# Values term of chunks 2 to 5 in 128x32 tiles, values loaded once more, tokens put in order at the eviction of y

## The chip, the cores and the metric

One core of one Trainium2 chip runs the kernel. The metric is the device time in microseconds (us), the median of repeated runs; lower is better. A profile shows one execution from the first to the last instruction (its span). The engines are named as in the profile: PE (TensorE matmuls), PEld (TensorE weight loads), DVE (VectorE), ACT (ScalarE), POOL (GpSimd), SP (SyncE, which here only issues DMAs).

## The reference

A gated linear attention over 768 tokens, for 4 batch rows and 8 heads of width 48, feeds a bilinear feed-forward layer over its 3072 tokens:

```python
for t in range(S):
    state = alpha[:, :, t, :, None] * state + np.einsum('bhd,bhe->bhde', k[:, :, t], v[:, :, t])
    y[:, :, t] = np.einsum('bhd,bhde->bhe', q[:, :, t], state)
...
a = x @ w_a        # x: y of all heads side by side, 3072 x 384; w_a, w_b: 384 x 1536
b = x @ w_b
return (a * b @ w_out).astype(np.float32)
```

## The kernel before

**Chunks.** The work is cut into 6 chunks. A chunk is 256 tokens of 2 batch rows (u = 0, 1). Partition p holds the tokens 2p and 2p + 1 (called rank 0 and 1), so that a load has runs of 96 elements. The 256 tokens are two blocks of 128 (g = 0, 1), which lie on the partitions 0 to 63 and 64 to 127. The recurrence goes from block to block by a 48x48 state per head; inside a block it is written with matrices.

**The attention part of a chunk.** Logarithms of alpha (step ln) and their running sums give the decays: pair sums on POOL (L613, l2s), their split into parts on DVE (L623, R), the sums on PE (L633, AQ), exponentials on ACT (L667, E); the decay over a whole block comes for chunks 0 and 1 from small matmuls (`decay_pe`, L700). `mul` (L678, steps mq and mk) multiplies queries and keys by them into `QKp`. For chunks 2 to 5, `turn_dma` (L767, step T) transposes `QKp` into `kqT` with a DMA that SP issues. `scores` (L841, step D) makes keys times queries on PE in 64x64 tiles: output half g of the partitions, and in it 64 keys of one rank. `masked` (L846, M) or `unmasked` and `masked_in_place` (L850 and L854, Mc and Mm) turn them into the masked tile `m`. `state_pe` and `state_pe_both` (L799 and L812, K and K2) make keys times values, and `state` (L829, L830, k) updates the state. The output y of a batch row collects in two PSUM banks: `carried` (steps SB and SA) adds queries times old state, and `inner` (Y) adds values times `m`. Both go through `out_mm` (L865) in 64x64 tiles. `inner` takes 48 matmuls a batch row: 12 pieces of heads, 2 ranks, 2 blocks. It reads the values from `vx`, a copy of the loaded values that `vcast` (L785 on ACT, L787 on DVE, step v) spreads to 96 columns a head. `evac` (L900, L902, step X) copies y of one batch row, 128x768, from PSUM to `xT`. The 128 tokens of a block stand there with the even ones first.

**The feed-forward part.** `ff` (L919, steps a and b) multiplies 128 columns of w_a or w_b with `xT`, for one batch row (256 tokens) or both (`*`, 512 tokens), in three matmuls. `ff_as` (L925, as) copies a's product to SBUF; `ff_prod` (L933, pr) multiplies it with b's product, and its output pattern (`tokens`) puts the tokens back in order. `ff_o` (L941, o) multiplies with w_out, `ff_out` (L956, L958, ot) evicts, `store` (L974, st) writes to memory.

**The order of the work** is written by hand: the text `PROGRAM` lists all steps, each with its chunk, its arguments, a PSUM bank and the engine (V is DVE, S is ACT, P is POOL, Y is SP). Each engine carries out its own steps in the order of the text and waits for the data of others. PE's order mixes the attention of one chunk with the feed-forward part of the one before. SP issues transposes, some loads and all stores; POOL issues the other loads, among its own arithmetic (L613, L652). Loads have two buffers for each of q, k, v and alpha, and are issued one to two chunks ahead.

Of the kernel before, what the change touches and what calls it, by code (L numbers as in the profile page):

```python
# [41 lines left out]
0: b 2 1 0; pr 2 1; a 6 * 3; as 4 1; b 1 1 2
1: l2 1 V
0: pr 4 1; as 6 *
1: H 1 V
0: pr 1 1
1: A2 0 7
0: a 11 * 0; a 7 * 5; a 0 1 4
1: L 1 V
0: k 1 1 V  # L50
1: ra 1
0: as 11 *
1: lv 0 q V; E 0 i
0: as 0 1; b 6 * 0; b 11 * 3; a 8 * 4; pr 6 *; pr 11 *
2: ld a * P
0: b 0 1 1; as 8 *; a 3 1 6
1: E 0 b; lv 0 k V
0: a 10 * 2; pr 0 1
1: mq 0 V; ld v 1 P
0: b 8 * 4  # L60
1: A2 1 7
0: as 10 *; b 10 * 2; pr 8 *
1: E 1 b
0: as 3 1; as 7 *; b 9 * 3; b 3 1 0; b 7 * 1; a 9 * 6
2: ld q * P
1: v 0 S; lv 1 q V; mk 0 V
0: pr 10 *
1: mq 1 V; C 0 1 4
0: as 9 *
1: C 0 0 2  # L70
0: o 0 0 5; pr 7 *
1: dk * 6
2: ld k * P
3: ld v * P
0: cz 1 v P; pr 9 *
1: Ce 0 0 S; E 1 i; de *; lv 1 k P; Ce 0 1 V; D 0 1 1; D 0 0 3
0: pr 3 1
1: Mc 0 0; K2 0 0 7 0
0: o 1 0 6
1: mk 1 V; M 0 1  # L80
0: o 3 0 4; o 1 1 -; ot 1 S; c3 P
3: ld a * P
0: cs 1 0 P; o 3 1 -
1: k 0 0 V; k 0 1 V; Mm 0 0 V; SB 0 1; C 1 0 3; C 1 1 7
0: ot 3 S; o 0 1 -
1: Ce 1 0 V
2: ln *
1: v 1 V; D 1 0 3; Ce 1 1 S; K2 1 1 6 0; Y 0; SA 0
0: ot 0 V
1: k 1 0 V; D 1 1 6  # L90
0: o 2 0 5
1: M 1 0
2: l2 0 V
1: X 0 S; a 3 0 1; Mc 1 1
2: l2s 0 P; l2s 1 P
1: a 2 0 3; a 4 0 4
2: R 0
1: k 1 1 V; as 4 0
2: ra 1
1: as 3 0; b 4 0 7  # L100
0: o 2 1 -
1: as 2 0
0: ot 2 S
1: pr 4 0
2: R 1; lv 1 q P
1: b 3 0 6; b 2 0 7; a 5 0 2; pr 3 0; b 5 0 3; as 5 0; b 1 0 5; a 1 0 1; pr 5 0; pr 2 0; a 7 0 2; as 1 0; pr 1 0
2: AQ 3
1: SB 1 6
2: lv 0 k P
1: a 10 0 5  # L110
2: lv 1 k V; ra 0; ld v * P
1: Mm 1 1 V
2: E 1 b
1: as 10 0; b 10 0 0; pr 10 0
2: mq 1 V; E 1 i
1: as 7 0; b 7 0 1
2: E 0 b; E 0 i
1: a 0 0 5
0: st 3 Y
2: dr  # L120
1: SA 1; Y 1
2: mk 1 V
1: pr 7 0; a 11 0 0; a 6 0 3; b 6 0 2; X 1 S; b 11 0 4; a 2 1 6; as 6 0; a 3 1 7; as 11 0; b 2 1 1; pr 6 0
2: lv 0 q V
1: b 4 1 0; as 2 1
2: T 1
1: pr 11 0
2: dl
0: st 0 Y
1: a 0 1 2; pr 2 1  # L130
2: mq 0 V
1: b 3 1 3; b 0 0 6; as 3 1; as 0 0; b 0 1 7; pr 3 1; a 8 0 1; a 9 0 5
0: st 1 Y
1: b 8 0 3; b 9 0 4; pr 0 0; as 0 1
2: mk 0 V
1: a 4 1 2
3: ln *
1: a 9 1 6; pr 0 1; as 8 0; b 9 1 1
3: ra 1
1: b 10 1 7; pr 8 0; a 10 1 3; as 4 1; as 9 0; as 9 1; a 6 1 6; b 6 1 2; b 11 1 5; pr 4 1; as 10 1; pr 9 0; a 11 1 4; pr 10 1; pr 9 1; as 6 1  # L140
2: v 1 S
1: a 8 1 3; b 8 1 1; a 7 1 6; pr 6 1
3: l2 0 V
1: as 11 1
2: T 0
1: as 8 1; a 5 1 4
3: ra 0
1: as 5 1; a 1 1 2
2: v 0 V
4: ld a * Y  # L150
1: pr 11 1; as 7 1; pr 8 1
2: K2 * * 0 7; D 1 1 3; D 1 0 5
1: as 1 1; b 5 1 2; o 2 0 1
2: k * 0 V
1: pr 5 1
3: v 0 S; v 1 S
1: b 1 1 2
2: Mc 1 0; M 1 1
3: l2s 0 P; l2s 1 P
1: b 7 1 0; o 2 1 -; pr 1 1; o 3 0 4  # L160
# [12 lines left out]
0: cs 0 0 P
2: Mc 0 1
4: ln *
3: ld q * Y; ld k * Y
2: k * 1 V
3: AQ 2
2: Y 1; SA 1; Mm 0 1 V; Mm 0 0 V; Y 0; X 0 S
3: E 0 b  # L180
4: l2 0 V
2: X 1 V
1: o 0 1 -
2: b 1 * 6; a 1 * 5
3: E 1 b
4: ld k * Y
3: E 1 i
1: ot 0 S
3: E 0 i
4: l2s 0 P  # L190
2: a 0 * 0; b 0 * 1; as 0 *; as 1 *
3: lv 0 k P; lv 0 q P
2: a 5 * 7
1: st 3 Y
2: a 7 * 4
4: l2s 1 P
2: a 2 * 5
3: lv 1 q V; mq 1 V; lv 1 k V
2: pr 1 *
3: dr  # L200
2: pr 0 *
3: mk 0 V
4: ld q * Y
0: st 2 Y
2: as 5 *; a 6 * 6; b 6 * 2; as 7 *
3: mq 0 V
2: b 9 * 4; b 7 * 0
1: st 2 Y
3: dl
4: R 0  # L210
2: b 5 * 7
1: o 1 0 3
2: a 9 * 1; pr 7 *; as 6 *
3: T 0
2: pr 6 *
4: ra 0
2: pr 5 *; a 11 * 6
3: mk 1 V
2: as 9 *; a 3 * 0
4: lv 0 k V; lv 0 q V; R 1  # L220
2: as 2 *
1: o 1 1 -
2: as 11 *; a 8 * 5; b 11 * 2; a 4 * 7; b 2 * 1
3: T 1
1: ot 1 V
2: pr 9 *; as 8 *; pr 11 *; pr 2 *; b 8 * 3; b 4 * 5; as 4 *
5: ld a * Y
3: K2 * * 4 6
2: pr 8 *; as 3 *; pr 4 *
3: k * 0 V; D 0 0 2; Mc 0 0  # L230
2: b 3 * 1
4: ra 1
2: pr 3 *; b 10 * 5; a 10 * 0
3: D 1 0 1; D 1 1 3
2: as 10 *
3: k * 1 V; Mc 1 1
2: o 0 0 7; o 2 0 0
3: M 1 0
5: ln *
2: pr 10 *  # L240
4: lv 1 q P
3: SB 1 3; D 0 1 1; Mc 0 1
4: lv 1 k P
5: ld q * Y
1: st 0 Y
3: SB 0 5
2: o 2 1 -
3: Mm 1 1 V; Mm 0 0 V; Mm 0 1 V
4: ld v * P
2: ot 2 S; o 0 1 -  # L250
4: AQ 0; E 0 b; E 0 i
3: SA 0; Y 0; SA 1
4: E 1 b
3: Y 1
5: l2s 1 V
4: mq 0 V; mk 0 V
3: X 0 S; X 1 S
2: o 3 0 2; o 3 1 -
4: T 0
3: a 5 * 3  # L260
4: E 1 i; v 0 S
3: a 9 * 0
2: ot 3 S
3: b 5 * 6; a 6 * 5; as 5 *
2: st 2 Y
3: as 9 *
5: ld k * P; l2s 0 P
3: as 6 *
5: ra 1
4: mq 1 V  # L270
2: ot 0 S
3: a 0 * 1
4: mk 1 V
3: a 1 * 2
4: D 0 0 3
5: l2 0 V
1: st 1 Y
4: dr
5: R 0
3: pr 5 *  # L280
4: v 1 S; M 0 0
3: b 1 * 7; as 1 *; a 3 * 5; b 9 * 6; pr 9 *; b 6 * 4; a 2 * 0; pr 6 *
4: T 1
5: lv 0 k P
3: b 0 * 6; as 0 *; as 2 *
4: dl
3: a 8 * 1
5: lv 1 q P
3: b 4 * 0; a 4 * 4; b 2 * 3; pr 1 *; pr 0 *; as 8 *; pr 2 *; as 4 *; pr 4 *; b 3 * 6; b 8 * 2
5: ld v * P; lv 1 k P  # L290
3: a 11 * 1
5: ra 0
3: as 3 *; pr 8 *; as 11 *; a 7 * 0
4: D 1 0 3; K * 0 5
5: lv 0 q P
3: pr 3 *; as 7 *
5: v 1 V
4: k * 0 V
# [106 lines left out]
def kernel(  # L405
# [14 lines left out]
    C = 128  # L420
# [678 lines left out]
```

## Time and profile before

| | |
|---|---|
| runs | 193.73, 194.18, 194.41 us; median 194.18 |
| span of the profiled execution | 192.0 us |
| first matmul starts, last one ends | 1.19 us, 188.65 us |
| DVE busy, ACT busy, POOL busy | 133.1, 106.5, 56.9 us |
| packets of DMA | 62618 in all, 18432 of them in POOL's queue |
| last load that lands | 120.2 us (values of chunk 5) |

The span is shorter than the time of a run, which holds the launch too: 2.2 us lie between the span and the median. "Busy" of PE counts the modelled time of a matmul from start to end, several at once; how fast PE advances is read from the starts, and matmuls of different tiles that start within a few ns of each other run side by side. A line of groups gives the line in the kernel, the engine, what it writes and reads with shapes, how often, busy time, mean time of one, and the idle time before.

### The profile page before, as it was taken

To read this page: it belongs to the slowest core of one execution; us is meant where nothing else is said; L and a number is where in the kernel's file an instruction comes from. 1 tells how busy PE (TensorE), PEld (TensorE's weight loads), DVE (VectorE), ACT (ScalarE), POOL (GpSimd) and SP (SyncE) were. 2 spreads that over 40 slices of the span, in tenths; PEclk is the share of its full clock that TensorE was granted. 3 is DMA by queue.
4 is the path that set the end of the run, shared out by engine and by line. 5 is a ranking of instruction groups with operands and counts; after the bars stand their busy time and mean duration, and the time that the engine had idled before them with its cause. 6 is when DMAs were issued, how large, how long until landed. Compare 5 with 4: busy or idle time off the path is not lost.

```text
span 192.0 us, 6086 instructions
## 1 busy us (share of the span) xinstructions
PE 186.8 (97%) x2613; PEld 116.9 (61%) x2613; DVE 133.1 (69%) x223; ACT 106.5 (55%) x194; POOL 56.9 (30%) x75
## 2 busy tenths in 40 slices
PE   7999999999999999999999999999999999999992
PEld 3888875677778876645557444656465644545562
DVE  2387698994989888899897956887567446252510
ACT  4448885656779867753487756743572435314211
POOL 8999626752450500640074262000000000000000
PEclk9999999999999999999999999999999999999999
DMA  5999999999969999999999989017641200000422
GB/s 132 274 219 218 251 253 235 244 269 264 251 107 166 165 216 265 248 254 149 233 213 181 156 174 129 3 42 140 146 66 44 85 0 0 0 0 3 164 82 82
DMA packets 62618, 29.40 MB, mean 153 GB/s; under 512 B 53712, under 2 KB 60768, under 8 KB 62592
## 3 DMA queue, kind: packets, MB, share of 16 engines
q0 software_dynamic: 18432, 13.37, 39.6%
q1 hardware_dynamic: 44016, 15.55, 38.1%
q8 instruction: 20, 0.33, 0.7%
q10 hardware_dynamic: 144, 0.10, 0.2%
q14 instruction: 6, 0.05, 0.1%
HBM read 25.98 MB, written 4.74 MB: 160 GB/s over the span
## 4 chain that ended last, share of the span: by engine, by line
PE 91%; DMA 5%; SPq 1%; DVE 1%; issue 1%; ACT 0%; DVEq 0%
PE psum L919 47%; PE psum L941 24%; PE psum L865 7%; PE psum L841 3%; DMA kqT<-QKp 3%; DMA q_t<-in_q_dram 3%; PE psum L736 2%; PE psum L633 1%; PE psum L952 1%; SPq L549 1%; PE psum L799 1%; PE psum L812 1%; PE psum L700 1%; PE psum L591 1%; PE psum L592 1%
## 5 line engine op out<-in xcount | busy, mean ns | idle before, releaser
L919 PE MATMUL psum<-xT,wb_t 128*128 128x512 bf16 (+1 forms) x270 | 56.0, 337 | 0.0
L919 PE MATMUL psum<-xT,wa_t 128*128 128x512 bf16 (+1 forms) x270 | 56.0, 337 | 0.0
L941 PE MATMUL psum<-wo_t,prod 128*128 128x384 bf16 x276 | 49.4, 326 | 0.0
L919 PEld LDWEIGHTS <-wb_t 128*128 128x128 bf16 x270 | 25.9, 98 | 19.9 <-issue 0.5
L919 PEld LDWEIGHTS <-wa_t 128*128 128x128 bf16 x270 | 25.9, 98 | 19.7 <-issue 0.3
L941 PEld LDWEIGHTS <-prod 128*128 128x128 bf16 x276 | 25.9, 98 | 17.6
L956 ACT ACTIVATE ot<-psum 128x384 f32<-128x384 f32 (+1 forms) x16 | 7.7, 482 | 22.7 <-PE psum L941 21.6
L850 ACT ACTIVATE m<-psum 128x1024 bf16<-128x1024 f32 x14 | 14.1, 1023 | 4.6 <-PE psum L841 4.3
L613 POOL TENSOR_TENSOR l<-la 64x384 f32<-64x384 f32 x7 | 7.8, 1108 | 26.6 <-ACT la L556 19.0
L846 DVE TENSOR_TENSOR m<-psum,mask 128x1024 bf16<-128x1024 f32 x10 | 12.1, 1220 | 3.1 <-PE psum L841 3.1
L652 POOL TENSOR_TENSOR q_t<-q_t,ra 128x384 f32<-128x384 f32 x5 | 6.1, 1215 | 22.5 <-ACT ra L645 19.7
L556 ACT ACTIVATE la<-a_t 128x1536 f32<-128x1536 f32 (+2 forms) x9 | 9.5, 1055 | 2.3 <-DMA a_t<-in_alpha_dram 2.2
L678 DVE TENSOR_TENSOR QKp<-q_t,beta 128x768 bf16<-128x768 f32 x10 | 10.0, 995 | 1.0 <-ACT beta L667 1.0
L865 PE MATMUL psum<-m,vx 64*64 64x128 bf16 x576 | 10.5, 217 | 0.0
L900 ACT ACTIVATE xT<-psum 128x768 bf16<-128x768 f32 x9 | 7.2, 816 | 5.7 <-PE psum L865 5.5
L678 DVE TENSOR_TENSOR QKp<-k_t,invb 128x768 bf16<-128x768 f32 x10 | 9.7, 972 | 0.8 <-ACT invb L667 0.8
L854 DVE TENSOR_TENSOR m<-m,mask 128x1024 bf16<-128x1024 bf16 x14 | 9.3, 684 | 1.2 <-ACT m L850 1.2
L958 DVE COPY ot<-psum 128x384 f32<-128x384 f32 (+1 forms) x9 | 4.8, 532 | 7.6 <-PE psum L941 4.7
L865 PEld LDWEIGHTS <-vx 64*64 64x64 bf16 x576 | 9.0, 107 | 0.5 <-issue 0.3
L841 PE MATMUL psum<-kqT 64*64 64x128 bf16 x384 | 9.0, 219 | 0.4 <-DMA kqT<-QKp 0.3
L652 POOL TENSOR_TENSOR k_t<-k_t,a_t 128x384 f32<-128x384 f32 x6 | 7.4, 1228 | 6.1 <-issue 3.3
L549 POOL DMA_DIRECT2D v_t<-in_v_dram x8 | 8.5, 1058 | 0.1
(271 smaller groups left out, 287.9 us busy)
## 6 DMA issues: line engine op xcount, KB each, us to landing
out_dram<-ot SPq DMA_DIRECT2D x23, 192.0 KB, 3.8
q_t<-in_q_dram SPq DMA_DIRECT2D x3, 768.0 KB, 6.5
a_t<-in_alpha_dram POOLq DMA_DIRECT2D x2, 768.0 KB, 15.2
k_t<-in_k_dram POOLq DMA_DIRECT2D x2, 768.0 KB, 12.1
v_t<-in_v_dram POOLq DMA_DIRECT2D x4, 384.0 KB, 7.0
a_t<-in_alpha_dram SPq DMA_DIRECT2D x2, 768.0 KB
k_t<-in_k_dram SPq DMA_DIRECT2D x2, 768.0 KB
a_t<-in_alpha_dram POOLq DMA_DIRECT2D x3, 384.0 KB, 8.5
```

What stands on the lines that cost most here:

```text
L549: eng.dma_start(out=t[:, us, hs].rearrange("p b h r d -> p (b h) (r d)"), in_=src[ch.b0 + us.start:ch.b0 + us.stop, hs, ch.s * 2 * C:(ch.s ...
L556: nc.scalar.activation(out=ch.la[:, us, hs].rearrange("p b h r d -> p (b h r d)"), in_=ch.a[:, us, hs].rearrange("p b h r d -> p (b h r d) ...
L613: eng.tensor_add(ch.l2[(1 - g) * HC:(2 - g) * HC, 1], x[:, :, 0, :], x[:, :, 1, :])
L652: eng.tensor_mul(x, x, by)
L678: eng.tensor_mul(QKp[ch.c % 2][:, u, j, :, hs, :D], src[:, u, hs].rearrange("p h r d -> p r h d"), f)
L841: nc.tensor.matmul(s2[g * HC:(g + 1) * HC, r, p, rk, :], lhsT=turned_part(ch, u, 1, rk, 2 * h + p, g, rs), rhs=queriesT(ch, u, 2 * h + p, ...
L846: nc.vector.tensor_mul(m.rearrange("p r a k s -> p (r a) (k s)"), ch.s2[u, h].rearrange("p r a k s -> p (r a) (k s)"), maskn(4))
L850: nc.scalar.activation(out=m.rearrange("p r a k s -> p (r a) (k s)"), in_=ch.s2[u, h].rearrange("p r a k s -> p (r a) (k s)"), func=AF.Copy)
L854: eng.tensor_mul(x, x, maskn(4))
L865: nc.tensor.matmul(y[c * DP:(c + 1) * DP, g, j // 2 * C:(j // 2 + 1) * C], lhsT=lhsT, rhs=rhs, start=(g, c) not in begun, stop=False, skip ...
L919: nc.tensor.matmul(p, lhsT=(wa_t, wb_t)[w][:, kk, f * 128:(f + 1) * 128], rhs=ch.xT[:, kk, us, :], start=(kk == 0), stop=(kk == KT - 1))
L941: nc.tensor.matmul(op, lhsT=ch.prod[:, f, at:at + C], rhs=wo_t[:, f, :], start=(f == 0), stop=(f == NFF - 1))
```

## The change

1. For chunks 2 to 5 (`NR = 2`), the scores are laid out so that all 128 keys of a block stand on the 128 partitions (rank 0 on 0 to 63, rank 1 on 64 to 127). `inner_rows` then takes both ranks in one matmul of 128 rows and 32 columns: 32 a batch row instead of 48. `scores` issues the same matmuls in another order of rank and block; the masks use a table `mask2`, made once on POOL (step cm2).
2. The values in that order are loaded once more (`load_rows`, step lw): four DMAs a chunk, issued by POOL, each for one block and one rank, with runs of 48 elements. They land in the memory of `vx`, seen as `vps` with 64 columns a head, whose padding is set to zero once (cz w). The state matmuls of these chunks read the loaded values directly, and `vcast` goes away for them.
3. `evac` now takes one block, 128x384, and writes its tokens in order; `xT` has the block as its outer index. `ff_prod` writes straight through.
4. `PROGRAM` is written anew: the same steps, but for those above, in another order, with other banks and partly other engines.

```diff
+    VP = D + DP // 2
+    NR = 2
...
+    mask2 = cst.tile([C, 2, HC], BF16, name="mask2")
+    vps = [t.rearrange("p b r h e -> p (b r h e)")[:, :4 * H * VP].rearrange("p (g b h e) -> p g b h e", g=2, b=2, h=H) for t in vxs]
...
+    def const_mask2(eng):
+        for rk in range(2):
+            ks = slice(rk * HC, (rk + 1) * HC)
+            ENG[eng].tensor_copy(mask2[ks], mask[ks, rk])
...
+    def load_rows(ch, g, rk, eng):
+        at = ch.s * 2 * C + g * C
+        eng.dma_start(out=vps[ch.c % 2][rk * HC:(rk + 1) * HC, g, :, :, :D].rearrange("p b h d -> p (b h) d"),
+                      in_=v[ch.b0:ch.b0 + 2, :, at:at + C, :].rearrange("b h (s r) d -> r s (b h) d", r=2)[rk])
...
+    def values(ch, gs, u, rk, hd):
+        return ch.v[gs, u, hd, rk, :] if ch.c >= NR else vxs[ch.c % 2][gs, u, rk, hd, :D]
...
+    SLICES = [(h, 3 * (h // 2) + j) for h in range(H) for j in ((0, 1) if h % 2 == 0 else (1, 2))]
+    RANKS = [[x for x in SLICES if x[1] % 4 == c] for c in range(4)]
+
+    def inner_rows(ch, u):
+        y, begun = ch.y[u]
+        vp = vps[ch.c % 2].rearrange("p g b h e -> p g b (h e)")
+        W32 = DP // 2
+        for n in reversed(range(len(SLICES) // 4)):
+            for g in range(2):
+                for c in range(4):
+                    h, j = RANKS[c][n]
+                    at = h * VP + W32 * j - D * h
+                    assert (g, c // 2) in begun
+                    nc.tensor.matmul(y[c * W32:(c + 1) * W32, g, j // 4 * C:(j // 4 + 1) * C], lhsT=vp[:, g, u, at:at + W32],
+                                     rhs=ch.m[u, h // 4][:, h % 2, h // 2 % 2, g, :], start=False, stop=False, skip_group_check=True)
...
-    def evac(ch, u, eng):
+    def evac(ch, u, g, eng):
         if not hasattr(ch, "xT"):
-            ch.xT = wk.tile([128, KT, B, C], BF16, name="xT")
-        o_ = ch.xT[:, :, 2 * u:2 * u + 2, :].rearrange("p a g s -> p g a s")
-        i_ = ch.y[u][0][:, :, :KT * C].rearrange("p g (a s) -> p g a s", a=KT)
...
+            ch.xT = wk.tile([128, B, KT, C], BF16, name="xT")
+        evict(ch.xT[:, 2 * u + g].rearrange("p a (s r) -> p a r s", r=2),
+              ch.y[u][0][:, g, :KT * C].rearrange("p (a r s) -> p a r s", a=KT, r=2), eng)
...
-        o_, a_, b_ = tokens(ch.prod[:, f, :], us), columns(a[:, :n], n), columns(b, n)
-        nc.vector.tensor_mul(o_, a_, b_)
+        nc.vector.tensor_mul(ch.prod[:, f, us.start * C:us.stop * C], a[:, :n], b)
```

The steps of the attention of chunk 3 in the new text, for example (steps of other chunks between them are left out):

```
3: lw 0 0 P
...
3: lw 0 1 P; lw 1 0 P
...
3: lw 1 1 P
...
3: l2s 0 P; l2s 1 P; R 0
...
3: AQ 2
...
3: ld q * Y
...
3: E 1 i; lv 1 q V; E 1 b; mq 1 V; E 0 b
...
3: ld k * Y; lv 0 k P; mk 0 V; lv 1 k V; mk 1 V
...
3: lv 0 q P; mq 0 V; dl
3: K2 * * 2 5
...
3: T 0
...
3: T 1
...
3: D 0 1 2; D 1 1 4; Mc 1 1; D 1 0 6; M 1 0
```

More of the change, by code (lines that the diff above doesn't have):

```diff
@@ L95 @@
[L95 to L100, printed above, removed]
+0: cz 1 v P
+1: mq 0 V
+0: b 10 * 0
+1: E 0 i; ra 1
+0: as 3 1; a 9 * 2; a 4 1 4; as 10 *; pr 10 *
+1: v 0 S; lv 0 k V; mk 0 V
+0: a 7 * 6
+1: de *
+0: a 11 * 5
+1: lv 1 q V
+0: pr 3 1; b 11 * 0; as 11 *; pr 11 *
+1: A2 1 1; E 1 b; C 0 0 5; E 1 i; mq 1 V; Ce 0 0 V
+0: as 4 1; b 7 * 7; b 4 1 0; pr 4 1; as 7 *; pr 7 *; b 9 * 1; as 9 *
+1: lv 1 k P; mk 1 V
+0: pr 9 *; a 6 * 4; as 6 *
+1: C 0 1 2; Ce 0 1 S; D 0 0 5; Mc 0 0; K2 0 0 0 7
@@ new lines @@
+0: pr 6 *
+1: k 0 0 V; k 0 1 V
+0: o 0 0 4; o 3 0 2
+1: D 0 1 5; Mm 0 0 V
+0: c3 P
+3: ld a * P
+1: SB 0 0
+2: ln *; ra 1
+1: C 1 0 3; Ce 1 0 V; M 0 1
+2: ra 0
+1: C 1 1 7; Ce 1 1 V
+0: cs 1 0 P; o 0 1 -; o 3 1 -; ot 3 V; st 3 Y
+1: D 1 0 5; Y 0; M 1 0; SA 0; X 0 1 S
+0: ot 0 S
+1: D 1 1 2; Mc 1 1
+0: o 1 0 7; o 2 0 1
+1: X 0 0 V; a 1 0 0; as 1 0
+2: l2s 0 P
+1: b 7 0 6; b 1 0 2
+0: o 1 1 -; ot 1 S
+2: l2 0 V; l2s 1 P
+0: st 0 Y
+2: R 0; R 1; AQ 4; E 0 b
+1: pr 1 0
+2: E 0 i
+1: v 1 V; K2 1 1 0 2; k 1 0 V
@@ L197 @@
[L197 to L202, printed above, removed]
+2: D 0 0 4; Mc 0 0
+3: l2s 0 P; l2s 1 P; R 0
+2: M 1 1
+1: o 0 1 -; ot 0 S; pr 9 1; o 2 1 -; ot 2 V
+2: D 0 1 2; Mc 0 1
+3: R 1
+2: SB 1 4; SB 0 6; Mm 0 0 V; Mm 0 1 V
+1: a 11 1 0; as 11 1; o 3 0 1; b 11 1 0; pr 11 1
+2: SA 0; SA 1
+3: AQ 2
+4: ln *; l2 0 V
+2: Y 1; Y 0; X 0 0 S
+1: o 1 0 0; o 1 1 -
+2: X 1 0 V
+1: o 3 1 -
+2: X 0 1 V; X 1 1 V; b 11 * 4
+3: ld q * Y
+2: a 11 * 5
+3: E 0 i
+0: cs 0 0 P
+4: l2s 0 P
@@ L241 @@
+2: a 1 * 3; b 1 * 1
+3: k * 0 V
+2: as 1 *; pr 1 *; as 0 *; b 4 * 4
+1: ot 1 V
+2: b 6 * 2; pr 6 *
+4: ra 1; l2s 1 P
+3: T 0
+4: R 0
+3: k * 1 V
+2: a 7 * 6; a 10 * 0; pr 0 *
+3: T 1
+2: b 10 * 1; a 4 * 2; as 10 *; pr 10 *; b 7 * 3; as 7 *; pr 7 *
+5: ld a * Y
+2: as 4 *; a 8 * 5; as 8 *; pr 4 *; a 9 * 0; as 9 *
+4: ra 0
+2: b 8 * 1; pr 8 *
+1: st 2 Y
+3: D 0 1 2; D 1 1 4; Mc 1 1; D 1 0 6; M 1 0
+2: b 9 * 0
 4: lv 1 q P
-3: SB 1 3; D 0 1 1; Mc 0 1
+2: pr 9 *
 4: lv 1 k P
 5: ld q * Y
-1: st 0 Y
@@ new lines @@
+5: ln *
+4: ld v * P; R 1; AQ 6; E 0 b
+3: Mm 1 1 V
+4: lv 0 k V
+3: SA 0
+1: st 0 Y
+3: SA 1
+4: E 0 i
+3: Mm 0 0 V; Y 0
+4: lw 0 0 P
+3: X 0 1 S
+4: lv 0 q V; mq 0 V
+3: Y 1
+2: o 3 0 6; o 3 1 -
+3: X 1 0 V; X 0 0 S; X 1 1 V; a 5 * 2; as 5 *
+4: E 1 b
+3: a 8 * 3
+5: l2 0 V
+3: b 6 * 4
+4: lw 0 1 P
+2: ot 2 S
+4: E 1 i
+2: ot 3 S
+4: lw 1 0 P
+3: a 6 * 2; as 6 *
+5: l2s 1 V
+3: b 1 * 1
+4: lw 1 1 P
+3: b 5 * 5
+4: mk 0 V; T 0
+5: ld k * P
+4: mk 1 V
+3: as 8 *; pr 6 *; pr 5 *; a 3 * 2; as 3 *
@@ L918, in ff @@
         for kk in range(KT):
[L919 removed]
+            nc.tensor.matmul(p, lhsT=(wa_t, wb_t)[w][:, kk, f * 128:(f + 1) * 128], rhs=ch.xT[:, us, kk, :], start=(kk == 0), stop=(kk == KT - 1))
     def ff_as(ch, f, us):
```

535 lines of the change are left out of this document (197 added, 338 removed).

## The prediction

> **What bounds the kernel.** I read the page's busy times and slices first.
>
> ```profile
> span 192.0 us, 6086 instructions
> PE 186.8 (97%) x2613; PEld 116.9 (61%) x2613; DVE 133.1 (69%) x223; ACT 106.5 (55%) x194; POOL 56.9 (30%) x75
> ...
> PE   7999999999999999999999999999999999999992
> ...
> DVE  2387698994989888899897956887567446252510
> ...
> DMA  5999999999969999999999989017641200000422
> ```
>
> PE has no hole from the first slices to the last. The waits, filtered to PE, confirm it:
>
> ```profile
> PE psum L574 <- DVE og L472: 1.2, 1, 1.2
> PE psum L841 <- DMA kqT<-QKp: 0.3, 1, 0.3
> PE psum L736 <- DVE QKp L678: 0.2, 1, 0.2
> ```
>
> After the warm-up PE waits 0.5 us in all, 0.3 of it for a transposing DMA. So the time is the sum of PE's work; a saving on PE counts in full, and a saving elsewhere counts only as cover. The same slices show two other resources without much room: the DMA engines (9 tenths or more from 5 to 110 us, save one slice) and DVE (7 to 9 tenths from 24 to 110 us, save one). The question is whether the change overdraws one of them.
>
> PE's timeline gives the price of the changed term:
>
> ```profile
> 75.20 0.65 PE L941 MATMUL psum<-wo_t,prod 128*128 128x384 bf16 x3
> 75.79 0.36 PE L633 MATMUL psum<-l,utb 64*64 64x384 bf16 x4
> ...
> 76.32 0.90 PE L865 MATMUL psum<-m,vx 64*64 64x128 bf16 x48
> 77.03 0.22 PE L865 MATMUL psum<-kqT,S 64*64 64x128 bf16 x1
> ...
> 77.20 0.85 PE L865 MATMUL psum<-m,vx 64*64 64x128 bf16 x48
> 77.99 1.15 PE L941 MATMUL psum<-wo_t,prod 128*128 128x384 bf16 x6
> ```
>
> From start to start, the 48 matmuls of one `inner` take 77.03 - 76.32 = 0.71 us: 12 sets of four tiles side by side, 59 ns a set. The second `inner` takes 0.79 to the first matmul of another tile shape, so a change of shape costs 0.08; on the way in, three 384-column matmuls take 0.59 where three of the 163 ns between such starts make 0.49, so 0.10.
>
> **PE, step by step.** Removed: 8 `inner` (4 chunks, 2 batch rows) of 0.71 = 5.7 us. Added: 8 times 32 matmuls, 8 sets of four. No row has a 128x32 tile. Best bound: a set costs what it costs now, 59 ns, since 128 columns stream either way: 8 x 8 x 59 ns = 3.8 us, saving 1.9. Worst bound from this neighbour, the only row with tiles of 128 rows and fewer columns:
>
> ```profile
> L700 PE MATMUL psum<-og,la 128*48 128x2 f32 x64 | 1.8, 186 | 0.0
> L865 PE MATMUL psum<-m,vx 64*64 64x128 bf16 x576 | 10.5, 217 | 0.0
> ```
>
> Its 32 matmuls of one batch row start within 0.91 us, 28 ns each with a new weight load each; 256 of those are 7.2 us, a loss of 1.5. I take 59 ns a set: the 64x64 row has the same 128 columns and four tiles at once, the other is fp32 with 2 columns, where a floor per matmul shows.
>
> Added too: changes of tile shape. Listing the shapes in both PE orders gives 61 runs before and 66 after: four because the 128x32 matmuls stand behind 64x64 ones, one from new places. At 0.08 to 0.10 each, 0.5 us (bounds 0 and 1.0, twice the row). All other PE instructions are the same in number and shape. The scores' order of rank and block still gives four different tiles in a row, and `xT` now feeds a 512-column matmul in four runs of 128; L841 already streams two runs of 64 at full pace, so 0. PE's sum: -1.9 + 0.5 = -1.4 us.
>
> **ACT and DVE.** ACT loses 6 of 9 `vcast` (850 ns each, 5.1 us), replaces 9 evictions of 816 ns by 12 of about 490 (nearest: L956, the same 384 columns) for -1.4, and gives one L742 (1.0) and one L956 (0.5) to DVE: -8 us. DVE gains 12 evictions of 554 (L958, the same 384 columns) for 3 of 952: +3.8; the two moved ones +1.2; two `vcast` less -0.7: +4.3. Against it, `ff_prod` stops writing with a stride: it takes 728 ns for 512 columns, while L902 and L846 (952 for 768, 1220 for 1024) put a straight 512 at about 690; 54 full and 36 half products, 0 to 40 ns each, save 0 to 3 us. I take half: DVE +3 us in all. The cover is DVE's idle time. Windows of 12 us from 48 to 108 have it busy 10.84, 10.64, 10.32, 11.33 and 10.57, so 6.3 us of 60 are free, and about 1.5 of the 3 fall there. Without that cover PE would wait for a PSUM bank that `ff_prod` frees, up to 1.5 us.
>
> **DMAs.** POOL issues 16 more, 1024 packets each (64 partitions, 16 runs), 16384 in all on 62618. A load of 1024 packets holds POOL 0.9 us (L549's shorter rows), so 14.4 us on 56.9 busy; behind them in POOL's order stand the next chunk's l2s and level steps. POOL is idle from 55.5 to 62.5 and from 65.2 to 77.2 us, and the l2s that would come some 2 us late feeds a DVE step at 71 us, so I cost the issuing at nothing. The packets matter more. The closest are those of v_t, cast to 192 bytes: 36 to 38 ns each, but two at a time; in the middle of a load 440 start in 0.5 us, 18 ns an engine, and over a whole load 27. The new ones write 96 bytes: 18 to 37 ns, so chunk 2's and 3's eight DMAs take 8192 / 16 x 18 = 9.2 to 18.9 us; I take 18, because the queue stays full and loads overlap at their ends. [...] They start when POOL has issued v_t of chunk 3 (54.3 us) and PE is done with chunk 0's values, about 56 us, just where the SP queue gets dense. What they push is this:
>
> ```profile
> 81.00 0.37 SPq L549 DMA_DIRECT2D q_t<-in_q_dram  x1
> ...
> 85.61 5.54 SPq L767 DMA_TRANSPOSE kqT<-QKp  x2
> ```
>
> k_t of chunk 3 lands at 78.8 us (its packets), `mul` of it ends at 85.55, the two transposes land near 90.7 and 94, and PE comes to these scores at 95.1 and 97.5: about 4 us of slack. Summed over the new PE order at the paces above, they stand at about 96 us and together. What takes up the 9.2 us: 4 of slack; 2.8, because chunk 2's AQ stands 4 us earlier in PE's order and its transposes go out that much sooner; 1.7 for three stores (0.56 each) that leave this stretch; and some 2 of idle DMA time at 59, 62 and 67 us. That is 10.5, so it just fits: 0. For chunk 4 the transpose was 0.3 us late already (111.50); its place in the new order is as tight, 0 to 1, and I keep the 0.3. Chunk 5's four DMAs fall at 118 to 130 us, where the DMA digits are 9, 0, 1: hidden.
>
> **Sum.** 192.0 - 1.9 + 0.5 = 190.6 us of span. The profiled execution lies 2.2 us under the median of the runs, so 192.8 us.
>
> **Rivals.**
> (1) Late transposes, slower: the eight new DMAs do not fit. From 10.5 us on, that is above 20.5 ns a packet, PE stands at chunk 3's scores by the excess. At the whole-load price of 27 ns they take 13.8, PE waits 3.3, and the time is 192.8 + 3.3 = 196.1; at 37 ns, 8.4 and 201.2. For it: the DMA digits of 9 and the slack of 4. Against it: the 18 ns at the middle of a load.
> (2) The tiles do not run four at once, slower: if weight loads wait for the running matmul, each set costs its 59 ns and a load of 107 (L865's PEld row): 64 x 0.107 = 6.8 more, 199.6. Against it: the 128*128 rows load weights (98 ns) under matmuls that start 109 ns apart for 256 columns, with the same rows of the array in use. [...]
> (3) No change: the saving is there, but the changes of shape cost the double (0.5 more), and DVE's 1.5 us in the crowded windows show in part (0.5): 192.8 + 1.0 = 193.8.
>
> **How the numbers follow.** Forecast 0.52, rival 1 0.29, rival 2 0.07, rival 3 0.12. What cannot be told from no change is 0.3%, 0.6 us. Forecast is faster, rivals 1 and 2 slower, rival 3 same: 0.52, 0.12, 0.36. Low end: 192.8 less the 0.3 of stall, less the 0.5 of shape changes, less 64 sets of 46 ns instead of 59 (46 lie between the last start of a set and the first of the next in the trace, which is all that stays if the four start at once), 0.8: 191.2. The high end takes in rival 1 to 28 ns a packet, 197.0. The forecast's own range is 191.2 to 193.6.
>
> **What would show it.** Right: the 128x32 matmuls in sets of four, 59 ns apart, `inner` at 0.47 us; PE's waits still under 1 us; 54 straight products under 710 ns. Rival 1: a PE wait on kqT at 95 to 100 us, and 96-byte packets above 20 ns. Rival 2: 128x32 starts more than 100 ns apart from set to set. I am wrong beyond all if PE waits at places that none of this names, since most steps are placed anew and I followed only the transposes and evictions.

## The result, and the profile after

The changed kernel takes 199.94 us (median of 4 runs, 199.64 to 200.12); the kernel before took 194.3 us on the same chip. The ratio is 1.0293, with a 95% interval of 1.0274 to 1.0312: slower by 5.7 us, where 192.8 us had been forecast. Of the runs below, 1, 6, 8 and 11 each had one slow execution among four, which their medians and ratios leave out; run 1's profile is of that one (granted clock 0.855, span 214.8 us), and no view of it is used. The profiled execution has a span of 198.3 us. Its page, busy times and slices:

```profile
span 198.3 us, 5841 instructions
...
PE 187.5 (95%) x2484; PEld 115.3 (58%) x2485; DVE 139.9 (71%) x232; ACT 98.9 (50%) x189; POOL 71.5 (36%) x95
...
PE   7989999999999989998999799989999999999993
...
DMA  5999999999999999995999995998592120001133
```

PE has some 130 matmuls fewer to do than before (2484 records against 2613), and yet behind its first slice its line now has digits of 7 and 8 where it had none, and the DMA line stays at 9 some slices longer. The waits, filtered to PE (in all, times, longest, in us):

```profile
PE psum L931 <- ACT invb L643: 1.4, 1, 1.4
PE psum L910 <- DVE prod L923: 1.2, 3, 0.6
PE psum L550 <- DVE og L434: 1.2, 1, 1.2
PE psum L822 <- DMA kqT<-QKp: 1.0, 1, 1.0
PE psum L879 <- DVE m L837: 1.0, 1, 1.0
```

Behind the warm-up (L550) PE waits 6.1 us, smaller groups that are not shown included, where it waited 0.5. (In the new file L910 is `ff`, L931 `ff_o`, L822 `scores`, L879 `inner_rows`, L837 the mask in place, L643 the exponentials, L628 the products with alpha's levels, L654 `mul`, L743 the transposing DMA, L520 the other loads, L525 the second load.) The longest stops are at 73.5, 109.8 and 132.0 us (start of the last matmul ahead of them). The chain of waits, pieces in order of time (start, duration, what), shows how they hang together:

```profile
59.75 2.46 POOL vx L525 x3
63.07 2.41 POOL vx L525 x3
65.48 9.16 DMA vx<-in_v_dram
74.64 10.72 DMA k_t<-in_k_dram
85.50 1.01 POOL k_t L628
86.53 1.73 DVE QKp L654
...
98.37 10.69 DMA a_t<-in_alpha_dram
109.20 1.35 issue
111.46 2.11 PE psum L931 x12
```

Before, the chain was PE's for 91% of the span; here it leaves PE for the second load, and then for the loads that came behind it: keys that SP issued at 74.64 land at 85.36 (chunk 3's landed at 78.8 before), the product with alpha follows on POOL, then `mul` on DVE, then chunk 3's transposes. SP's timeline has the next link:

```profile
92.66 5.61 SPq L743 DMA_TRANSPOSE kqT<-QKp  x2
98.37 0.53 SPq L520 DMA_DIRECT2D a_t<-in_alpha_dram  x1
```

SP issues chunk 5's alpha only behind those late transposes. On ACT, the logarithm of chunk 5 (step ln) waits for it, and two exponentials of chunk 4 stand behind the logarithm. ACT's timeline (the bracket is the idle time ahead):

```profile
109.16 1.48 ACT L532 ACTIVATE la<-a_t 128x1536 f32<-128x1536 f32 x1 [3.05 <-DMA a_t<-in_alpha_dram]
110.55 0.47 ACT L643 ACTIVATE beta<-psum 128x384 f32<-128x384 f32 x1
110.92 0.48 ACT L643 ACTIVATE invb<-psum 128x384 f32<-128x384 f32 x1
```

They read the PSUM bank into which PE's next output step writes, so PE stands until 111.46. The DMAs issued at 60 us have become a stop 50 us later, through several queues. Run 11 below has the same order without the second load: there SP issues these keys at 68.61 us and chunk 5's alpha at 95.81, and PE does not stop at this place.

### The profile page after: what moved, and what is told of

It is laid out like the page before. It is cut to its first block, busy times and chain, and to the rows that moved or that the text cites. A ratio compares the mean times of both kernels' runs of the same rounds, so it can differ in the third digit from the quotient of the medians.

```text
span 198.3 us, 5841 instructions
## 1 busy us (share of the span) xinstructions
PE 187.5 (95%) x2484; PEld 115.3 (58%) x2485; DVE 139.9 (71%) x232; ACT 98.9 (50%) x189; POOL 71.5 (36%) x95
## 4 chain that ended last, share of the span: by engine, by line
PE 58%; DMA 20%; POOL 10%; DVE 7%; issue 3%; ACT 1%; SPq 0%; POOLq 0%; DVEq 0%; ACTq 0%
PE psum L910 34%; PE psum L931 16%; DMA k_t<-in_k_dram 5%; DMA a_t<-in_alpha_dram 5%; DMA vx<-in_v_dram 5%; DMA wb_t<-in_moe_w_b_dram 4%; POOL vx L525 3%; DVE prod L923 2%; PE psum L848 2%; PE psum L822 2%; DVE m L837 1%; DVE QKp L654 1%; PE psum L942 1%; PE psum L712 1%; POOL v_t L520 1%
## 5 line engine op out<-in xcount | busy, mean ns | idle before, releaser
L910 PE MATMUL psum<-xT,wb_t 128*128 128x512 bf16 (+1 forms) x270 | 55.6, 337 | 1.7 <-DVE prod L923 1.2
L910 PE MATMUL psum<-xT,wa_t 128*128 128x512 bf16 (+1 forms) x270 | 55.2, 336 | 0.0
L931 PE MATMUL psum<-wo_t,prod 128*128 128x384 bf16 x276 | 49.2, 326 | 1.9 <-ACT invb L643 1.4
L910 PEld LDWEIGHTS <-wb_t 128*128 128x128 bf16 x270 | 25.5, 98 | 22.2 <-issue 2.1
L931 PEld LDWEIGHTS <-prod 128*128 128x128 bf16 x276 | 26.2, 98 | 19.9 <-issue 2.2
L910 PEld LDWEIGHTS <-wa_t 128*128 128x128 bf16 x270 | 25.9, 98 | 19.8 <-DVE xT L948 0.4
L946 ACT ACTIVATE ot<-psum 128x384 f32<-128x384 f32 (+1 forms) x15 | 7.1, 480 | 16.3 <-PE psum L931 15.6
L525 POOL DMA_DIRECT2D vx<-in_v_dram x16 | 13.1, 837 | 0.3 <-POOL vx L480 0.3
L654 DVE TENSOR_TENSOR QKp<-q_t,beta 128x768 bf16<-128x768 f32 x10 | 10.1, 1011 | 3.3 <-ACT beta L643 3.1
L628 POOL TENSOR_TENSOR k_t<-k_t,a_t 128x384 f32<-128x384 f32 x6 | 6.8, 1133 | 14.3 <-issue 7.5
L948 DVE COPY ot<-psum 128x384 f32<-128x384 f32 (+1 forms) x10 | 5.4, 537 | 9.2 <-PE psum L931 6.3
L654 DVE TENSOR_TENSOR QKp<-k_t,invb 128x768 bf16<-128x768 f32 x10 | 10.3, 1041 | 2.1 <-POOL k_t L628 1.2
L837 DVE TENSOR_TENSOR m<-m,mask 128x1024 bf16<-128x1024 bf16 x14 | 11.0, 799 | 0.7 <-ACT m L833 0.7
L822 PE MATMUL psum<-kqT 64*64 64x128 bf16 x384 | 9.2, 220 | 1.4 <-DMA kqT<-QKp 1.0
L628 POOL TENSOR_TENSOR q_t<-q_t,ra 128x384 f32<-128x384 f32 x5 | 5.6, 1121 | 12.4 <-ACT ra L621 12.1
L948 DVE CAST xT<-psum 128x384 bf16<-128x384 f32 x12 | 6.5, 581 | 3.7 <-PE psum L879 2.8
L822 PEld LDWEIGHTS <-kqT 64*64 64x64 bf16 x384 | 6.4, 106 | 4.6 <-issue 2.8
L520 POOL DMA_DIRECT2D v_t<-in_v_dram x8 | 8.5, 1065 | 0.7 <-DVE vx L763 0.5
```

What stands on the lines that cost most here:

```text
L520: eng.dma_start(out=t[:, us, hs].rearrange("p b h r d -> p (b h) (r d)"), in_=src[ch.b0 + us.start:ch.b0 + us.stop, hs, ch.s * 2 * C:(ch.s ...
L525: eng.dma_start(out=vps[ch.c % 2][rk * HC:(rk + 1) * HC, g, :, :, :D].rearrange("p b h d -> p (b h) d"), in_=v[ch.b0:ch.b0 + 2, :, at:at + ...
L628: eng.tensor_mul(x, x, by)
L654: eng.tensor_mul(QKp[ch.c % 2][:, u, j, :, hs, :D], src[:, u, hs].rearrange("p h r d -> p r h d"), f)
L822: nc.tensor.matmul(s2[half * HC:(half + 1) * HC, r, p, part_, :], lhsT=turned_part(ch, u, 1, rk, 2 * h + p, g, rs), rhs=queriesT(ch, u, 2 ...
L837: eng.tensor_mul(x, x, maskn(ch, 4))
```

## The experiments

Each was run beside the kernel before on one chip; that kernel's median was 193.8 to 193.9 us in these runs and 194.3 beside the changed kernel. Since chips differ by that much, runs are compared by their ratios, of 194 us: 0.001 is 0.19 us, and with four runs a side a difference of two ratios is known to about 0.5 us. "Theory A" is the second load, "theory B" the new order, "theory C" the evictions and masks.

**Run 1, no second load.** All `lw` steps taken out of the new order:

```diff
-2: lw 0 0 P; lw 0 1 P
...
-5: lw 1 1 P
```

> The changed kernel without its sixteen DMAs of the values (the padded tiles keep what chunks 0 and 1 left in them, so the values term of chunks 2 to 5 is computed from old values; every other instruction stays). Theory A (the second load is what costs: its packets push back the transposes and the loads of chunks 4 and 5, and its issuing on POOL stretches VectorE): the stalls of TensorE at 73.5, 90, 110 and 132 us shrink, and the time falls from 199.9 to 192.5 to 194.0. Theory B (the new order is worse whatever is loaded): the stalls stay, 198 or more. Theory C (the evictions by blocks and the mask on VectorE): 198 or more too, with waits of TensorE for VectorE and ScalarE rather than for DMAs.

195.77 us, ratio 1.0102 (1.0085 to 1.0119), between the ranges of theory A and theory B. From 1.0102 to 1.0293 are 1.91%, 3.7 us of the 5.7: that is the load, less than theory A had it. 2.0 us remain although the tiles are in.

**Run 4, the same sixteen DMAs with a sixteenth of the packets.**

```diff
-        eng.dma_start(out=vps[ch.c % 2][rk * HC:(rk + 1) * HC, g, :, :, :D].rearrange("p b h d -> p (b h) d"),
+        eng.dma_start(out=vps[ch.c % 2][rk * HC:(rk + 1) * HC, g, 0, 0, :D],
...
```

> The changed kernel with all sixteen DMAs issued at their places, each with one head of one sequence, 64 packets instead of 1024 (the rest of the padded tiles keeps old values). Theory A by packets: the transposes and the loads are no longer late, 193 to 194.5, though POOL issues as often. Theory A by issuing: POOL beside VectorE is what costs, 197 or more, with VectorE's multiplications of 681 ns still stretched to over 1000 beside the issues. Theory B: 198 or more.

196.29 us (ratio 1.0132, 1.0115 to 1.0149), again between the ranges: 1.0293 - 1.0132 makes 3.1 us for the packets, and 0.6 is left for the issuing (against run 1), though 16 issues still hold POOL 8.4 us (13.1 with all packets). PE's waits in it:

```profile
PE psum L550 <- DVE og L434: 1.2, 1, 1.2
PE psum L879 <- DVE m L837: 1.1, 1, 1.1
PE psum L910 <- DVE prod L923: 0.6, 2, 0.4
```

The waits for kqT and invb are gone with the packets; the one for `m` is not. The windows from 60 to 72 us (length, busy time and number on PE, PEld, DVE, ACT and POOL, clock, DMA share summed over the queues, GB/s), first of the changed kernel, then of run 4:

```profile
60.00:72.00 12.00, 12.00 (x180) 10.35 (x179) 10.29 (x24) 8.32 (x20) 8.41 (x11) 1.00 1.76 137
```

```profile
60.00:72.00 12.00, 12.00 (x179) 10.26 (x178) 10.29 (x25) 7.68 (x19) 5.36 (x9) 1.00 1.04 186
```

With all the 96-byte packets the packets' times, several at once, add up to 1.76 of the DMA engines' time, and 137 GB/s are moved; with a sixteenth of them it is 1.04 and 186. The engines are busier and bring less.

**Run 2, both edits in the old order; run 6, the old kernel with the load alone.** In run 2 the DMAs stand where the casts stood; run 6 sends them to a tile that nothing reads.

```diff
+2: lw 0 0 P; lw 0 1 P
...
+5: lw 1 0 P; lw 1 1 P
```

> Both edits of the computation in the order of the kernel before: evictions by blocks, 128x32 tiles in chunks 2 to 5, and the sixteen DMAs where the value casts of these chunks stood. Theory A: the load crowds the same transposes and loads, so this is slower than before, 196 to 200. Theory B: with the old order the tiles bring their 1.9 us and little is lost, 192 to 193.5. Theory C: slower than before by what the evictions cost, 195 to 197, and the same without the load.

> The kernel before, unchanged in its computation, with sixteen more DMAs of the same 1024 packets into tiles that nothing reads, issued behind its value casts. If the load by itself delays the transposes and loads (theory A): 198 to 203, with the wait of TensorE for the transposes of chunks 2 and 4 that the second run showed (4.5 and 3.2 us). If the DMAs only hurt where something waits for the values themselves: 194.0 to 195.0.

203.8 us (1.0447 to 1.0554) and 205.22 us (1.0521 to 1.0605), both more than theory A had. The load alone costs 10.9 us in the old order; PE's waits in run 2:

```profile
PE psum L887 <- DMA kqT<-QKp: 4.5, 1, 4.5
PE psum L861 <- DMA kqT<-QKp: 3.2, 1, 3.2
```

So the new order does hide part of the load: it makes 3.7 us of what is 9.3 (run 2 against run 5 below) or 10.9 in the old one. Not all of the old order's price is waiting. The window from 72 to 84 us of run 2 has a granted clock of 0.72 (third number from the end):

```profile
72.00:84.00 12.00, 7.52 (x96) 4.02 (x98) 5.33 (x9) 3.81 (x4) 0.00 (x0) 0.72 1.36 224
```

The trace's clock is at 0.5 from 76.6 to 83.5 us, and the 4.5 us stop ends at 77.8. The 5.7 us at half clock behind it make some 2.8 us (an estimate), which no wait shows. The changed kernel's trace has no such stretch.

**Run 3, evictions alone, old order and tiles** (`NR = 99`, each `X u e` made two steps).

> The order and the tiles of the kernel before, with the first edit alone: y is evicted by blocks in token order and the products are straight. Theories A and B: no stall comes or goes, 193.5 to 194.8 against 194.2. Theory C: over 195.5, with longer waits of TensorE for y's evictions or for VectorE.

194.04 us, 1.0008 (0.9993 to 1.0024): nothing. Theory C falls for the evictions; run 5 below, which has the new masks too, stays at 1.0021.

**Run 5, both edits, old order, no load; run 12, the same with the values terms of a chunk side by side.** Chunk 3's steps, for example:

```diff
-3: SA 0; Y 0; SA 1
+3: SA 0; SA 1; Y 0; Y 1
...
-3: Y 1
```

> Both edits of the computation in the order of the kernel before, without the sixteen DMAs (the values term of chunks 2 to 5 reads what chunks 0 and 1 left). What the tiles bring where nothing is loaded: if eight inner terms of 0.47 instead of 0.71 us are worth 1.9 us, as the prediction's second step has it, 192.0 to 192.8 against 194.0 for the evictions alone. The rival, that the tiles gain little because the sets wait for each other or for masks that come late: 193.5 or more.

> The fifth run (both edits, old order, no second load) with the two values terms of each of chunks 2 to 5 put side by side behind the second carried term, so that TensorE changes between 64x64 and 128x32 tiles once a chunk and not twice. In the fifth run's trace the last 64x64 matmul before 128x32 tiles and the last 128x32 one before 64x64 tiles took 146 and 150 ns where they took 46 with one shape. If that is what took the tiles' gain: 8 changes of 0.10 us fewer, 193.4 to 193.8 against 194.3. If not: 194.2 to 194.6.

194.34 us (ratio 1.0021, 1.0002 to 1.0041) and 193.64 us (0.9985, 0.9967 to 1.0003). Run 5 came out where the rival had it, but for another reason. PE's timeline (start, busy time, what) of the values terms of chunk 3, in run 3 with the old tiles:

```profile
104.31 0.84 PE L886 MATMUL psum<-m,vx 64*64 64x128 bf16 x48
104.98 0.22 PE L886 MATMUL psum<-kqT,S 64*64 64x128 bf16 x1
```

in run 5:

```profile
104.34 0.22 PE L879 MATMUL psum<-kqT,S 64*64 64x128 bf16 x1
104.34 0.22 PE L879 MATMUL psum<-kqT,Sm 64*64 64x128 bf16 x1
104.49 0.63 PE L910 MATMUL psum<-m,vx 128*32 128x128 bf16 x32
105.05 0.24 PE L879 MATMUL psum<-kqT,S 64*64 64x128 bf16 x1
```

and in run 12:

```profile
104.81 1.08 PE L907 MATMUL psum<-m,vx 128*32 128x128 bf16 x64
105.82 0.66 PE L959 MATMUL psum<-wo_t,prod 128*128 128x384 bf16 x3
```

With the old tiles a values term lasts 0.67 us to the next start, of the same shape as its neighbours. In run 5 it lasts 0.56, and 0.10 more pass ahead of it: the last 64x64 matmul is followed after 146 ns instead of 46, since the shape changes. That takes the whole gain. In run 12 both terms together take 1.01 us and change shape once in and once out. From run 5 to run 12 8 changes fell away (68 runs of one shape became 60), and 0.70 us with them, about the 0.8 expected.

**Runs 7, 9, 10 and 13, the padded tiles filled on the chip.** Four copies of 64 partitions a chunk from the values already loaded stand in for the four DMAs:

```diff
+    def rows_copy(ch, g, rk, eng):
+        o_ = vps[ch.c % 2][rk * HC:(rk + 1) * HC, g, :, :, :D].rearrange("p b h d -> p (b h) d")
+        i_ = ch.v[g * HC:(g + 1) * HC, :, :, rk, :].rearrange("p b h d -> p (b h) d")
...
-3: v 0 S; v 1 S
+3: vw 0 0 S; vw 1 1 S; vw 0 1 S; vw 1 0 S
```

> Both edits in the order of the kernel before, but the padded tiles are filled on the chip: four copies of 64 partitions and 768 elements from the value tile already loaded, two where each cast of 128 partitions stood, on the same engine as that cast. No second load. A copy on VectorE should take the 350 ns of a cast, on ScalarE 850, so VectorE gains 0.7 us of work and ScalarE 5.1 in the whole run. If the load was what ate the gain of the tiles: 192.0 to 193.2, faster than both kernels. If the copies delay ScalarE's other work: 193.5 to 195.

> A version meant to beat both kernels: the seventh run (both edits, old order, padded tiles filled by copies on the chip) with the values terms paired as in the run before, and the two evictions of a sequence shared between ScalarE and VectorE in chunks 2 to 5 and for sequence 1 of chunk 0. By the paired tiles 0.8 us and by the waits of TensorE for evictions in chunk 0 up to 0.5 us from 194.6: 193.0 to 193.8. If VectorE becomes late: 194.5 or more.

> As the run before, with the four copies of a chunk issued later, between its state and its carried terms, two on ScalarE and two on VectorE (0.85 and 0.35 us each), so that ScalarE's copies no longer stand ahead of the products' operands (TensorE waited 0.5 us for those in the seventh run). 192.8 to 193.6 if that was it; as the run before or slower if the copies now come late for the values terms.

> The twelfth run (both edits, old order, paired values terms, evictions on one engine a sequence, 193.6 without any load) with the padded tiles filled by four copies a chunk from the loaded values, put at places where the twelfth run's trace shows ScalarE idle for 2.5 us or more and VectorE for 0.5 or more (ScalarE 3, 3, 3 and 2 of 0.85 us in chunks 2 to 5, VectorE the rest of 0.35). If the copies fit into these holes: 193.4 to 194.0, the first complete kernel with the tiles that is not slower than before. If they shift other work of ScalarE: 194.4 or more.

Run 7 took 194.56 us (1.0013 to 1.0055), run 9 194.99 (1.0053 to 1.0084), run 10 195.55 (1.0079 to 1.0112). None of the three came under the kernel before: in run 9 PE waited 1.0 us for evictions that I had moved to DVE, and 0.5 for an ACT copy of an operand behind a value copy; in run 10 1.0 again, and 0.7 for an eviction of the output on ACT. Run 13 leaves the evictions on their engines and puts the copies where run 12's trace shows both engines idle: 193.21 us, ratio 0.9971 (0.9949 to 0.9992). That is a little under the 193.4 to 194.0 expected. It computes the whole reference and is faster than both kernels; against the old one the difference is small, 0.3%, and the interval reaches 0.1%. Its page:

```profile
span 191.1 us, 5851 instructions
...
PE 184.8 (97%) x2484; PEld 114.5 (60%) x2485; DVE 134.2 (70%) x229; ACT 112.9 (59%) x208; POOL 58.0 (30%) x79
```

ACT has 14 us more to do than in the changed kernel, PE's waits are 1.8 us behind the warm-up.

**Run 11, no load, and two steps of chunk 5 moved from POOL to DVE.**

```diff
-5: lv 1 k P
+5: lv 1 k V
...
-5: lv 0 q P
+5: lv 0 q V
```

> The changed kernel without its second load (the first run, 195.9; values of chunks 2 to 5 old), and two multiplications of chunk 5 moved from POOL to VectorE (k by alpha of one sequence, q by the ratio of the other), which in the fourth run ran beside the masks of chunk 4 while these took 1621 and 1484 ns instead of 684, and TensorE waited 1.1 us. If that meeting is the new order's own loss: 194.4 to 195.0, masks back at 684 ns. If not: 195.6 or more.

194.96 us (ratio 1.0072, 1.0052 to 1.0092), by the ratios 0.6 us less than run 1, and at the upper edge of what was expected. In the changed kernel, DVE's and then POOL's timeline at that place:

```profile
130.22 2.89 DVE L837 TENSOR_TENSOR m<-m,mask 128x1024 bf16<-128x1024 bf16 x2
```

```profile
128.11 3.28 POOL L525 DMA_DIRECT2D vx<-in_v_dram  x4
131.37 1.19 POOL L628 TENSOR_TENSOR k_t<-k_t,a_t 128x384 f32<-128x384 f32 x1
132.54 1.43 POOL L628 TENSOR_TENSOR q_t<-q_t,ra 128x384 f32<-128x384 f32 x1
```

and the group of these masks in the changed kernel and in run 11 (times, busy time, mean ns):

```profile
L837 DVE TENSOR_TENSOR m<-m,mask 128x1024 bf16<-128x1024 bf16 x14 | 11.0, 799 | 0.7 <-ACT m L833 0.7
```

```profile
L814 DVE TENSOR_TENSOR m<-m,mask 128x1024 bf16<-128x1024 bf16 x14 | 9.4, 686 | 0.7 <-ACT m L810 0.7
```

Two masks of 684 ns took 1482 and 1487 beside POOL, and PE's wait for `m` at 132 us (1.0 us) follows. In run 11 all 14 are back at 686 and the wait is gone. Run 4 shows what stretches them. There both masks (1621 and 1484 ns) lie beside POOL's two products; its timeline, DVE and then POOL:

```profile
126.00 3.03 DVE L837 TENSOR_TENSOR m<-m,mask 128x1024 bf16<-128x1024 bf16 x2
```

```profile
123.90 2.13 POOL L525 DMA_DIRECT2D vx<-in_v_dram  x4
125.99 1.07 POOL L628 TENSOR_TENSOR k_t<-k_t,a_t 128x384 f32<-128x384 f32 x1
126.96 1.51 POOL L628 TENSOR_TENSOR q_t<-q_t,ra 128x384 f32<-128x384 f32 x1
```

The issuing of DMAs alone did not stretch such masks: in run 2 three of them, at 108.19, 108.79 and 109.81 us, took 680, 681 and 692 ns while POOL issued DMAs throughout. (In the changed kernel the first mask lies, by the records, for most of its time beside the last two issues; that stays unexplained.) The meeting is thus shown for the kernels that issue the load, where four issues stand ahead of the products in POOL's queue, 3.3 us in the changed kernel and 2.1 in run 4. Run 11 changes two things against them, the load and the engine of the products. Run 1 has the products on POOL and no issues ahead of them, and no profile shows whether they meet the masks there; so the cause of the 0.6 us between run 1 and run 11 is not shown. 1.7 us remain to run 12, which does the same work in the old order.

**Runs 14 and 15, old order up to 45 us, new order behind it,** without and with the load. The traces of runs 11 and 12, laid side by side by the matmul work done, stand 1.5 us apart at 54 us and no more behind it. These runs ask whether the old start takes that back.

> The steps of the old order up to the first output step of chunk 0 (about 45 us), and behind them all other steps in the new order; no second load, chunk 5's two multiplications on VectorE, as in the eleventh run (195.1), one feed-forward step of chunk 1 stands ahead of a values term instead of behind it. If the new order's own loss lies in the first two chunks: 193.8 to 194.4, five stops of TensorE between 25 and 54 us gone. If it lies behind them or is spread: 194.8 or more.

> The same, with the sixteen DMAs and POOL's two multiplications as in the changed kernel: its whole computation with the first 45 us in the old order. If the terms add up: 199.9 less what the run before gained on the eleventh run, some 198.7 to 199.2, with the stops at the scores of chunk 2, at chunk 3's output and at the masks of chunk 4 as in the changed kernel. If an earlier start lets the DMAs start earlier and hide: under 198.

195.56 us (ratio 1.0105, 1.0066 to 1.0144) and 198.12 us (1.0217, 1.0179 to 1.0254). Run 14 is not in the range that was hoped for, run 15 in neither of its two. The seam of run 14 made stops of its own, with 0.71 and 0.67 us from one matmul to the next ahead of 40.0 and 41.4 us, and in the profiled execution (the longest of the four, 197.01 us) a stretch at a granted clock of 0.5 follows, 41.4 to 44.8 us. The first matmuls behind the second stop show it:

```profile
41.42 3.74 PE L912 MATMUL psum<-wo_t,prod 128*128 128x384 bf16 x12 [0.48 <-ACT kqT L699]
```

Twelve of these take 1.95 us at full clock (changed kernel, 44.55 us). From there to the end the distance to run 12 stays at some 3 us (3.05 at 52 us, 2.85 at the end). So behind the first 45 us the new order, without the load, lost nothing against the old one; that its first 54 us cost some 1.5 us is read from two traces, but putting the old start back did not show it.

In run 15 the load and POOL's two products add 2.2 us to run 14, where they add 4.3 from run 11 to the changed kernel. The traces of runs 14 and 15, which have the same seam, lie level up to 118 us and are 1.7 us apart from 131 us on: PE stops for a transpose (0.6) and for the masks (1.0), and not at chunk 2's scores or chunk 3's output. The eight DMAs of chunks 2 and 3 had their packets under way from 59.3 to 69.1 us there, 19 ns a packet and engine, and cost nothing. So the cost of the load depends on what it meets, and the terms do not simply add.

**Run 8, new order with the old tiles and casts, no load.**

> The new order with the values term of the kernel before: no second load, no padded tiles, the casts of chunks 2 to 5 at the places of the DMAs, evictions by blocks kept (chunk 4's values terms stand some steps later, behind the next feed-forward steps, since their tiles need it). Theory B (the new order itself has lost about 4 us): 196.5 to 198.5, that is the run without the load plus the 1.9 us of the tiles. If the new order is as good as the old one and the tiles or their mask cost it: 193.5 to 195.0.

201.69 us (ratio 1.0371, 1.031 to 1.0432), over 3 us above what either theory had. Its trace shows ACT waiting 4.6 us for chunk 5's alpha, at the same place as the changed kernel and with no second load (SP issues it at 98.34 us, as there at 98.37). Probably the casts have no room in this order, which was not tested further. The run says nothing of the order by itself, but that this one place has little slack.

## Why the prediction was wrong, step by step

From run to run the difference splits like this:

| step | ratio to before | difference, us |
|---|---|---|
| evictions by blocks (run 3) | 1.0008 | +0.2 |
| tiles, terms paired, no load (run 12) | 0.9985 | -0.4 |
| new order, two products on DVE (run 11) | 1.0072 | +1.7 |
| these products on POOL (run 1), cause open | 1.0102 | +0.6 |
| the second load (changed kernel) | 1.0293 | +3.7 |

The forecast had -1.4 us, so it was 7.1 us off: 3.7 of the load, 2.3 of the new places, 1.0 of the tiles' saving that did not reach the time, and 0.2, with rounding.

- *The tiles, -1.9, and their changes of shape, +0.5: right in PE's work, and not in the time.* A set takes (1.010 - 0.152) / 15 = 57 ns, and a change of shape 0.10. The matmuls of the carried and values terms take 13.62 us from start to start in run 3 and 12.43 in run 12, so 1.2 less for the forecast 1.4. The forecast went on "a saving on PE counts in full"; in the time of the runs 0.4 us are seen (run 12 against run 3: 0.9985 and 1.0008), with a change of shape at both ends of each term none (run 5). PE's listed waits grew from 1.9 us in run 3 to 3.4 in run 12, which takes up the rest. Rival 2 fell: the sets start 57 ns apart (run 12, and the changed kernel, where a weight load takes 97 ns), so PE takes the next weights while the tiles run.
- *ACT and DVE, nothing: nearly right.* Straight products take 683 ns for 512 columns (690 assumed). The 128x384 evictions with their strided write take 599 ns on ACT, not 490, and 581 on DVE, not 554; run 3 shows that this has cover in the old order. DVE's busy time grew by 6.8 us, not by 3, and the masks' stretching is 1.6 of that; PE's waits for products are 1.2 us in the changed kernel and 0.6 in run 11.
- *The DMAs: the step that failed.* It read "That is 10.5, so it just fits: 0", with 18 ns a packet. Both sides of it were wrong. The eight DMAs of chunks 2 and 3 had their packets under way from 60.9 to 76.2 us: 15.3 us for 8192 / 16 = 512 packets an engine, 30 ns each, where 9.2 had been taken. In run 15 the same eight took 19 ns in another stretch; here SP's queue moved some 6600 packets in the same 15.3 us. And of the room of 10.5 us, 2.8 came from chunk 2's transposes going out sooner. AQ of chunk 2 started at 52.48 us instead of 54.23, but the transposes went out later than before, first the old kernel's, then the changed one's:

```profile
58.46 1.89 SPq L767 DMA_TRANSPOSE kqT<-QKp  x1
...
63.31 2.84 SPq L767 DMA_TRANSPOSE kqT<-QKp  x1
```

```profile
58.90 2.90 SPq L743 DMA_TRANSPOSE kqT<-QKp  x1
...
64.03 4.66 SPq L743 DMA_TRANSPOSE kqT<-QKp  x1
```

The second one's packets ran from 67.8 to 73.9 us (64.8 to 68.6 before), in the midst of the new DMAs. What followed is rival 1 in its direction and its cause, late transposes, but not in its place. PE did not stand at chunk 3's scores, but at chunk 2's, for that second transpose (1.0 us, 73.5), at products (0.6, 90.2), at an output step (1.4, 109.8) and at the masks (1.0, 132.0); of these run 11 has none but 0.3 us for products. I had followed the transposes of chunks 3 and 4 alone; chunk 2's second transpose, the keys and alpha loads in SP's queue, and what stands behind them on ACT were not in the sum. That rival 1's 3.3 us at 27 ns lies near the measured 3.7 is luck: at the measured 30 ns its rule gives 15.3 - 10.5 = 4.8 us, at a place where PE did not wait, and the 3.7 are of all sixteen DMAs. (By the same rule the high end of the range, 197.0, stands for 28.7 ns, not 28.)

- *The issuing on POOL at nothing: wrong by some 0.6* (run 4 against run 1, little more than their intervals). In run 4's trace PE waits 1.1 us for the masks that POOL's products stretch, and these stand behind the issues; no wait of PE goes back to the late l2s that I had considered.
- *The new places of the other steps at nothing: wrong by 2.3 us.* I had listed the matmuls of both orders by kind and found them the same. Their waits were not the same. 1.7 us are lost by about 54 us; PE's listed waits from 15 to 56 us are 1.3 us in run 11 and 0.7 in run 12, less than half of it, and the rest stays open. So does the cause of the 0.6 us between runs 1 and 11.

## What to carry to other kernels

What a DMA of short runs cost here depended on the stretch it fell into (the same eight DMAs took 30 ns a packet and engine in the changed kernel and 19 in run 15), and what such a DMA delays must be followed through every queue in which something stands behind it: here one load became a stop of PE by way of SP, POOL, DVE, SP again and ACT. Where the data is on the chip already, a few copies on idle engines can stand in for a second load, if their places are taken from a trace and not from where the old step stood. A new tile shape has to be priced with its neighbours: a values term between terms of another shape paid for two changes of about 0.10 us (run 5), so the terms of one shape were better side by side (run 12).

## What the runs showed of the hardware

- A change of tile shape on PE cost the same in both directions: 145 to 146 ns from the last 64x64 matmul to the first of 128x32 (10 of 11 times in runs 5 and 12), 146 to 152 from the last 128x32 to the next shape, where 43 to 48 ns passed inside one shape. The traces show this price of about 0.10 us, and not what happens in it.
- The whole loads of 96-byte packets took, in the changed kernel, 18 ns a packet and engine almost alone (chunk 5's), 30 while SP's queue was busy (chunk 2's and 3's), and 43 beside two loads at 104 to 116 us (chunk 4's). In the same trace a 96-byte packet took 29 ns (median) against 36 for v_t's 192 bytes, and in the densest half microsecond 741 of them started against 457, 11 and 18 ns an engine.
- The masks, DVE multiplications with both inputs in SBUF, took up to 2.4 times their time beside POOL's multiplications: 1621 and 1484 ns for 684 in run 4. A product with one input in PSUM did not: 0.69 us at 126.22 in the changed kernel, beside POOL's product from 125.78 to 126.96. What makes the difference is not shown. DMA issues on POOL alone left the masks at 680 to 692 ns (run 2).
- The granted clock of PE fell to 0.5 for some us around stops in four traces: 76.6 to 83.5 us in run 2 (a stop of 4.5 us), 117.8 to 128.1 in run 6 (6.5 us), and 41.4 to 44.8 in run 14 and 41.1 to 44.5 in run 15 (two stops of 0.5 us each). The changed kernel's stops of 1.0 and 1.4 us had none. What decides is not shown; the price comes on top of the wait and stands in no list of waits.
